# Fewer, larger pieces for the first and last loads of a decode attention kernel

## The chip, the cores and the metric

One core of a Trainium2 chip runs the kernel. The metric is device time in microseconds (us); less is better.

## The reference

One query for each of 16 heads attends to 8192 keys of width 256, all in bf16:

```
B, H, Sq, Sk, D = 1, 16, 1, 8192, 256
scores = einsum("bhqd,bhkd->bhqk", q, k) * D ** -0.5
p = softmax(scores, axis=-1)
out = einsum("bhqk,bhkd->bhqd", p, v)
```

K and V are 4 MB a head each, 134 MB together, and each byte is used once.

## The kernel before

A head's K and V lie in SBUF as 128 partitions of 64 rows: partition p holds rows 64p to 64p + 63, so that a "column" j (one of the 64) is one row of 256 numbers in each partition, 64 KB over all partitions. There are two buffers for K and two for V; even heads use the first, odd heads the second.

**Loads.** The list `stream` (lines 57 to 70) holds (K or V, head, first column, last column, semaphore) in the order of issue, and SP issues all of it on one queue (line 136). Before K of head h it waits until DVE has finished head h - 2 (line 133, semaphore `kd`), before V of head h until TensorE has finished the weighted sum of head h - 2 (line 135, `pv`). Heads 0 and 1 wait for nothing. A load in pieces has one semaphore for each piece. K0 comes as columns 0 to 15, 16 to 31 and 32 to 63. V0 and V1 come in halves, with K2 between the halves of V0 and K3 between the halves of V1. From head 2 on the list is K of head h + 2, then V of head h. V13 comes in halves, V14 in four pieces of 16 columns, V15 in nine pieces, the last two of 2 columns.

**Scores.** Of each head's 64 columns, DVE does the first 48 (`head`, lines 180 to 207): one multiply-and-sum a column (line 191), with a wait at the columns where a new piece of K0 begins (line 187). TensorE does the last 16 (`scores`): transposes (line 280), which ACT copies to SBUF (line 376), then matmuls with q (line 294). TensorE begins a head of even number only when all of K0 has come (lines 274 to 276). DVE then takes the maximum of each partition (line 207); TensorE transposes these (line 228), DVE takes the maximum of all (line 173), TensorE spreads it (line 234), and ACT takes the exponential (line 388). DVE's two small steps for other heads, `recips` and `xmax`, are put in between its columns (lines 217 and 218).

**Weighted sum.** `pv` (lines 252 to 269) is 64 matmuls, one a column of V, into one row of PSUM. It waits for the first piece of V, and at a column where a piece may begin it waits for that piece's semaphore. TensorE's code is a loop over pairs of heads with one body for all turns, so the waits for the pieces of V13, V14 and V15 stand in each turn. They compare with a register (`fin_turn`, `half_turn`, lines 348 and 349) that is 16 in all turns but the last, or last two, where it is 32; the semaphores start at 16, given by POOL (line 167). The order in a turn is scores of the even head, pv of the even head two before (with the small matmuls of the odd head in between at columns 32, 48 and 64), scores of the odd head, pv of the odd head two before (lines 351 to 366).

**Output.** ACT scales the row by the reciprocal of the sum (line 401) and issues its store (line 408).

Of the kernel before, what the change touches and what calls it, by code (L numbers as in the profile page):

```python
# [10 lines left out]

NPE = 16
GRP = 4
K_FIRST = (16, 32)
V_HALVED = 13
V_LATE = {14: (0, 16, 32, 48), 15: (0, 16, 28, 38, 46, 52, 57, 60, 62)}
AHEAD = {"kd": 1, "sc": 1, "sp": 2, "ex": 2, "m": 1, "g": 1, "mT": 1, "l": 2, "bc": 1, "nb": 1, "rc": 2, "pv": 2, "fin": 4}
V_SEMS = (("va0", "v0b", "v0c", "v0d"), ("va1", "v1b", "v1c", "v1d", "v1e", "v1f", "v1g", "v1i", "v1j"))


class _Step:
# [19 lines left out]
def bass_standalone__mha_softmax__decode_kernel(nc: bass.Bass, q: bass.AP, k: bass.AP, v: bass.AP, out: bass.AP):  # L41
    B, H, Sq, D = q.shape
    Sk = k.shape[2]
    P = 128
    J = Sk // P
# [3 lines left out]
    NG = NPE // GRP  # L49
    JD = J - NPE  # L50
    QW = D + NH
    HALF = J // 2
    dt = k.dtype

    stream = [("k", 0, 0, K_FIRST[0], "k0"), ("k", 0, K_FIRST[0], K_FIRST[1], "k0a")]
    stream += [("k", 0, K_FIRST[1], J, "k0b"), ("k", 1, 0, J, "k1")]
    stream += [("v", 0, 0, HALF, "va0"), ("k", 2, 0, J, "k0"), ("v", 0, HALF, J, "v0c")]
    stream += [("v", 1, 0, HALF, "va1"), ("k", 3, 0, J, "k1"), ("v", 1, HALF, J, "v1c")]  # L60
    for h in range(2, H):
        if h + 2 < H:
            stream.append(("k", h + 2, 0, J, f"k{h % 2}"))
        if h in V_LATE:
            for (a, b), name in zip(zip(V_LATE[h], V_LATE[h][1:] + (J,)), V_SEMS[h % 2]):
                stream.append(("v", h, a, b, name))
        elif h == V_HALVED:
            stream += [("v", h, 0, HALF, "va1"), ("v", h, HALF, J, "v1h")]
        else:
            stream.append(("v", h, 0, J, f"va{h % 2}"))  # L70

    with contextlib.ExitStack() as ctx:
# [39 lines left out]

        for name in ("qc", "pool", "cb", "cf", "qp", "qs", "qb", "kd", "tp", "kt", "sp", "sc", "m", "mT", "g", "bc", "nb", "ex"):
            sem(name)
        for name in ("l", "rc", "pv", "fin", "ldq", "k0", "k0a", "k0b", "k1", "va0", "va1", "v1h", "o0", "o1"):
            sem(name)
        late = [name for row in V_SEMS for name in row[1:] if name not in ("v0c", "v1c")] + ["v1h"]
        for row in V_SEMS:
            for name in row[1:]:
                sem(name)  # L120

        def src(t, h):
            return t[0, h].rearrange("(p j) d -> p (j d)", p=P)

        if True:
# [15 lines left out]
            @(lambda f: f(nc.gpsimd))  # L141
            def _(pool):
                def step(ins, n):
                    ins.then_inc(sem("pool"), 1)
                    pool.wait_ge(sem("pool"), n)

                def eye(t, n, done):
                    step(pool.memset(t[:, :], 0.0), n)
                    pool.affine_select(
                        out=t[:, :],  # L150
                        in_=t[:, :],
                        compare_op=ALU.not_equal,
                        fill=1.0,
                        base=0,
                        pattern=[[-1, P]],
                        channel_multiplier=1,
                    ).then_inc(sem(done), 1)

                eye(identb, 1, "cb")
                eye(ident, 2, "cf")  # L160
                pool.memset(ones_row[:, :], 1.0).then_inc(sem("cf"), 1)
                pool.memset(ones_col[:, :], 1.0).then_inc(sem("cf"), 1)
                pool.memset(q_all[:, H * QW : (H + 1) * QW], 0.0).then_inc(sem("cf"), 1)
                for name, n in AHEAD.items():
                    pool.nop().then_inc(sem(name), n)
                for name in late + ["o0", "o1", "va0", "va1"]:
                    pool.nop().then_inc(sem(name), 32 if name in ("o0", "o1") else 16)

            @(lambda f: f(nc.vector))
            def _(dve):  # L170
                def xmax(h):
                    dve.wait_ge(sem("mT"), h.of(1, 2))
                    dve.tensor_reduce(g[0:1, h.par : h.par + 1], mx[0:1, 0:P], AX.X, ALU.max).then_inc(sem("g"), 1)  # L173

                def recips(h):
                    dve.wait_ge(sem("l"), h.of(1, 3))
                    dve.wait_ge(sem("fin"), h.of(1, 3))
                    dve.reciprocal(recip[0:1, h.par : h.par + 1], qps[0:1, 0:1]).then_inc(sem("rc"), 1)  # L178

                def head(h, at):  # L180
                    dve.wait_ge(sem("qb"), h.of(1, 1))
                    dve.wait_ge(sem("ex"), h.of(1, 1))
                    dve.wait_ge(sem(f"k{h.par}"), h.of(8, 16 - 8 * h.par))  # L183
                    buf = kbuf[h.par]
                    for j in range(JD):
                        if j in K_FIRST and h.par == 0:
                            dve.wait_ge(sem("k0a" if j == K_FIRST[0] else "k0b"), 16)
                        if j == JD - 1:

                            dve.wait_ge(sem("sc"), h.of(1, 2))  # L190
                        ins = dve.tensor_tensor_reduce(  # L191
                            out=buf[:, j * D : (j + 1) * D],
                            in0=buf[:, j * D : (j + 1) * D],
                            in1=q_now[h.par][:, 0:D],
                            scale=SCALE,
                            scalar=0.0,
                            op0=ALU.mult,
                            op1=ALU.add,
                            accum_out=S[h.par][:, j : j + 1],
                        )  # L200
                        if j in at:
                            at[j]()
                    ins.then_inc(sem("kd"), 1)
                    if JD in at:
                        at[JD]()
                    dve.wait_ge(sem("kd"), h.of(1, 2))
                    dve.tensor_reduce(m[:, h.par : h.par + 1], S[h.par][:, :], AX.X, ALU.max).then_inc(sem("m"), 1)  # L207

                with dve.Fori(0, H // 2) as i:  # L209
                    ev, od = _Step(0, i), _Step(1, i)  # L210
                    prev = od.back(2)

                    def later(f, h):
                        with dve.If(i > 0):
                            f(h)

                    head(ev, {2: lambda: later(recips, ev.back(2)), 40: lambda: later(xmax, prev)})
                    head(od, {2: lambda: later(recips, prev), 3: lambda: xmax(ev)})
                last = _Step(H - 1)
                recips(last.back(1))  # L220
                xmax(last)
                recips(last)

            @(lambda f: f(nc.tensor))
            def _(pe):
# [23 lines left out]
                        stop=True,  # L249
                    ).then_inc(sem("l"), 1)  # L250

                def pv(h, waits, at):

                    pe.wait_ge(sem("fin"), h.of(1, 3))
                    pe.wait_ge(sem(f"va{h.par}"), h.of(8, 32 - 8 * h.par))
                    for j in range(J):
                        for name, value in waits.get(j, ()):
                            pe.wait_ge(sem(name), value)
                        ins = pe.matmul(  # L259
                            acc[h.par][0:1, 0:D],  # L260
                            lhsT=E[h.par][:, j : j + 1],
                            rhs=vbuf[h.par][:, j * D : (j + 1) * D],
                            start=(j == 0),
                            stop=(j == J - 1),
                        )
                        if j == J - 1:
                            ins.then_inc(sem("pv"), 1)
                        if j + 1 in at:
                            at[j + 1]()
# [75 lines left out]
                pe.wait_ge(sem("cf"), 4)  # L345
                with pe.Fori(0, H // 2 + 1) as i:
                    ev, od = _Step(0, i), _Step(1, i)
                    fin_turn = pe.snap((i // 8) * 16 + 16)
                    half_turn = pe.snap(((i + 1) // 8) * 16 + 16)
                    old = od.back(2)  # L350
                    with pe.If(i < H // 2):
                        scores(ev)
                    with pe.If(i > 0):
                        pv(
                            ev.back(2),
                            {V_LATE[14][n]: [(V_SEMS[0][n], fin_turn)] for n in range(1, len(V_SEMS[0]))},
                            {32: lambda: transpose_m(old), 48: lambda: bcast(old), 64: lambda: total(old)},
                        )
                    with pe.If(i < H // 2):
                        scores(od, before=ev)  # L360
                    with pe.If(i > 0):
                        waits = {V_LATE[15][n]: [(V_SEMS[1][n], fin_turn)] for n in range(1, len(V_SEMS[1]))}
                        waits[HALF] = [("v1h", half_turn)]
                        pv(old, waits, {})
                    with pe.If(i < H // 2):
                        total(ev)

# [121 lines left out]
```

## Time and profile before

| | us |
|---|---|
| median of 3 runs | 320.18 (320.08 to 320.52) |
| the profiled execution | 320.12 |
| its span, first to last instruction | 318.6 |
| busy, DVE | 275.2 |
| busy, TensorE matmuls | 219.2 |
| busy, ACT | 92.5 |
| mean DMA rate over the span | 421 GB/s read |

The span is told from the profile of one execution, whose own time stands beside it. Busy times overlap. In the timeline a row has the start in us, how long it took, the engine, the line, what it writes and reads, how many instructions are taken together, and in brackets how long the engine had been idle and what ended that. "PEld" is TensorE's weight loads, "SPq" and "ACTq" are the issues of DMAs on those engines' queues. In the DMA view a queue's row has packets, MB, and the time of the packets as a share of 16 engines' time; an issue's row has KB and us from the issue to the landing.

### The profile page before, as it was taken

Reading aid. Unit: us, or ns where it says so; the run is one execution under the profiler, and the core shown is the slowest. Engines: PE = TensorE matmul, PEld = TensorE weight load, DVE = VectorE, ACT = ScalarE, POOL = GpSimd, SP = SyncE. Lnnn points to the kernel's source line nnn. Section 1 sums busy time; section 2 is a strip of 40 time slices with the busy share of each in tenths; the row PEclk is TensorE's granted clock in tenths of the full one; section 3 lists DMA queues with packets and bytes.
Section 4 is the critical chain, followed back from the end, with each engine's and each line's share of the span. In section 5 each row is a group of like instructions: output and inputs, shape, how many; then the busy total and the mean of one; then the engine's idle time right before and its main releaser. Section 6 shows DMA issues by size and latency. Waiting matters only on the chain.

```text
span 318.6 us, 6833 instructions
## 1 busy us (share of the span) xinstructions
PE 219.2 (69%) x2163; PEld 156.0 (49%) x2163; DVE 275.2 (86%) x1584; ACT 92.5 (29%) x172; POOL 1.6 (0%) x11
## 2 busy tenths in 40 slices
PE   4446185988775947949387482975739668497987
PEld 1335163656553634727256262663626446266664
DVE  3989999999999898897988979799798897979920
ACT  5436050333215050330505114051330603306010
POOL 1000000000000000000000000000000000000000
PEclk9999999659797875957879597695977859699999
DMA  7999999999999999999999999999999999999995
GB/s 303 447 418 465 393 455 407 448 416 448 412 448 428 428 444 411 453 412 453 420 436 440 416 448 407 453 416 449 424 432 444 411 449 416 444 405 428 419 416 201
DMA packets 6981, 134.29 MB, mean 422 GB/s; under 512 B 800, under 2 KB 1216, under 8 KB 1856
## 3 DMA queue, kind: packets, MB, share of 16 engines
q1 hardware_dynamic: 6912, 134.22, 98.6%
q8 instruction: 2, 0.03, 0.0%
q10 hardware_dynamic: 64, 0.02, 0.0%
q14 instruction: 3, 0.02, 0.0%
HBM read 134.23 MB, written 0.01 MB: 421 GB/s over the span
## 4 chain that ended last, share of the span: by engine, by line
DMA 64%; PE 19%; DVE 15%; SPq 1%; issue 1%; ACT 0%; DVEq 0%; ACTq 0%
DMA vbuf<-in_v_dram 58%; PE acc L259 18%; DVE kbuf L191 14%; DMA kbuf<-in_k_dram 7%; SPq L136 1%; DVE S L191 0%; DVE g L173 0%; PE sm L234 0%; ACT o_sb L401 0%; DVE recip L178 0%; DVEq L209 0%; DVEq L183 0%; PE qps L244 0%; DVE m L207 0%; ACTq L400 0%
## 5 line engine op out<-in xcount | busy, mean ns | idle before, releaser
L191 DVE CUSTOM_DVE_ANT_0 kbuf<-kbuf,q_now 128x256 bf16<-128x256 bf16 x768 | 268.4, 409 | 21.3 <-DMA kbuf<-in_k_dram 20.4
L259 PE MATMUL acc<-vbuf,E 128*1 128x256 bf16 x1024 | 147.1, 313 | 41.6 <-DMA vbuf<-in_v_dram 41.4
L259 PEld LDWEIGHTS acc<-vbuf,E 128*1 128x1 bf16 x1024 | 95.5, 95 | 86.2 <-DMA vbuf<-in_v_dram 44.4
L376 ACT ACTIVATE KT<-tp 128x1024 bf16<-128x1024 bf16 x64 | 62.3, 1021 | 46.4 <-PE tp L280 45.9
L191 DVE DVE_READ_ACCUMULATOR2_ANT S<- 128x1 f32 x768 | 55.2, 72 | 0.0
L280 PE MATMUL tp<-identb,kbuf 128*128 128x128 bf16 x512 | 42.2, 239 | 14.7 <-DMA kbuf<-in_k_dram 14.5
L280 PEld LDWEIGHTS tp<-identb,kbuf 128*128 128x128 bf16 x512 | 33.6, 107 | 18.1 <-DMA kbuf<-in_k_dram 12.1
L294 PE MATMUL spe<-q_now,KT 128*128 128x1 bf16 x512 | 22.9, 166 | 27.3 <-ACT KT L376 27.0
L294 PEld LDWEIGHTS spe<-q_now,KT 128*128 128x128 bf16 x512 | 18.1, 99 | 35.7 <-ACT KT L376 26.1
L401 ACT ACTIVATE o_sb<-acc,recip 1x256 bf16<-1x256 f32 x16 | 7.3, 458 | 87.0 <-PE acc L259 85.7
L384 ACT ACTIVATE negb<-sm 128x1 f32<-128x1 f32 x16 | 2.8, 174 | 83.8 <-PE sm L234 83.8
L173 DVE TENSOR_REDUCE g<-mx 1x1 f32<-1x128 f32 x16 | 4.4, 276 | 7.5 <-PE mx L228 7.5
L234 PE MATMUL sm<-g,ones_row 1*128 1x1 f32 x32 | 6.5, 268 | 5.0 <-DVE g L173 5.0
L228 PE MATMUL mx<-ident,m 128*1 128x128 f32 x32 | 6.5, 287 | 4.3 <-DVE m L207 4.3
L234 PEld LDWEIGHTS sm<-g,ones_row 1*128 1x128 f32 x32 | 5.1, 198 | 7.1 <-DVE g L173 5.6
L371 ACT ACTIVATE q_now<-q_all 128x258 bf16 x16 | 6.7, 418 | 0.1
L178 DVE RECIPROCAL recip<-qps 1x1 f32<-1x1 f32 x16 | 2.4, 152 | 3.9 <-PE qps L244 3.9
L388 ACT ACTIVATE E<-S,negb 128x64 bf16<-128x64 f32 x16 | 5.6, 348 | 0.5
L336 PE MATMUL acc<-q_sb,identb 16*128 16x256 bf16 x16 | 4.3, 404 | 0.8 <-ACT q_all L426 0.8
L228 PEld LDWEIGHTS mx<-ident,m 128*1 128x1 f32 x32 | 2.1, 82 | 5.1 <-DVE m L207 4.8
L426 ACT ACTIVATE q_all<-acc 128x512 bf16<-128x512 f32 x8 | 4.3, 592 | 0.6 <-PE acc L336 0.6
L380 ACT ACTIVATE S<-spe 128x16 f32<-128x16 f32 x16 | 2.9, 184 | 3.6 <-PE spe L294 3.6
(24 smaller groups left out, 18.5 us busy)
## 6 DMA issues: line engine op xcount, KB each, us to landing
kbuf<-in_k_dram SPq DMA_DIRECT2D x15, 4096.0 KB, 20.3
vbuf<-in_v_dram SPq DMA_DIRECT2D x11, 4096.0 KB, 28.7
vbuf<-in_v_dram SPq DMA_DIRECT2D x6, 2048.0 KB, 24.4
vbuf<-in_v_dram SPq DMA_DIRECT2D x5, 1024.0 KB, 14.8
kbuf<-in_k_dram SPq DMA_DIRECT2D x2, 1024.0 KB, 5.8
kbuf<-in_k_dram SPq DMA_DIRECT2D x1, 2048.0 KB, 11.3
vbuf<-in_v_dram SPq DMA_DIRECT2D x1, 768.0 KB, 10.2
vbuf<-in_v_dram SPq DMA_DIRECT2D x1, 640.0 KB, 11.3
```

The lines of the kernel that those rows point to most:

```text
L173: dve.tensor_reduce(g[0:1, h.par : h.par + 1], mx[0:1, 0:P], AX.X, ALU.max).then_inc(sem("g"), 1)
L191: ins = dve.tensor_tensor_reduce(out=buf[:, j * D : (j + 1) * D], in0=buf[:, j * D : (j + 1) * D], in1=q_now[h.par][:, 0:D], scale=SCALE, ...
L228: pe.matmul(mx[0:1, 0:P], lhsT=m[:, h.par : h.par + 1], rhs=ident[:, :], start=True, stop=True).then_inc(sem("mT"), 1)
L234: pe.matmul(sm[:, 0:1], lhsT=ones_row[0:1, 0:P], rhs=g[0:1, h.par : h.par + 1], start=True, stop=True,).then_inc(sem("bc"), 1)
L259: ins = pe.matmul(acc[h.par][0:1, 0:D], lhsT=E[h.par][:, j : j + 1], rhs=vbuf[h.par][:, j * D : (j + 1) * D], start=(j == 0), stop=(j == J ...
L280: ins = pe.transpose(tp[gi % 2][:, b * D + hf * P : b * D + (hf + 1) * P], buf[:, j * D + hf * P : j * D + (hf + 1) * P], identb[:, :],)
L294: ins = pe.matmul(spe[:, c : c + 1], lhsT=KT[gi % 2][:, b * D + hf * P : b * D + (hf + 1) * P], rhs=q_now[h.par][:, D + hf : D + hf + 1], ...
L336: ins = pe.matmul(acc[pair % 2][:, (h % 2) * D : (h % 2 + 1) * D], lhsT=identb[0:H, h : h + 1].to_broadcast([H, P]), rhs=q_sb[:, :], start ...
L371: act.activation(out=q_now[h.par][:, :], in_=src_q, func=ACT.Copy).then_inc(sem("qb"), 1)
L376: act.activation(out=KT[gi % 2][:, :], in_=tp[gi % 2][:, :], func=ACT.Copy).then_inc(sem("kt"), 1)
L388: act.activation(out=E[h.par][:, :], in_=S[h.par][:, :], func=ACT.Exp, bias=negb[:, h.par : h.par + 1], scale=1.0, accum_out=lsum[:, h.par ...
L401: act.activation(out=o_sb[h.par][0:1, :], in_=acc[h.par][0:1, 0:D], func=ACT.Copy, scale=recip[0:1, h.par : h.par + 1],).then_inc(sem("fin ...
```

## The change

The first and last loads are cut differently. K0 comes as columns 0 to 15 and 16 to 63. V0 and V1 come whole, so that the list begins K0 (two pieces), K1, V0, K2, V1, K3, K4, V2, K5, V3. V13 comes in 34 and 30 columns, V14 in 24, 20 and 20, V15 in 20, 14, 10, 8, 6, 4 and 2. The waits for pieces compare with the constant 16 in all turns: POOL gives each of their semaphores 16 for each turn but those in which a load gives it, and the first matmul of each piece takes 16 back. The registers `fin_turn` and `half_turn` go.

```
-K_FIRST = (16, 32)
-V_HALVED = 13
-V_LATE = {14: (0, 16, 32, 48), 15: (0, 16, 28, 38, 46, 52, 57, 60, 62)}
+K_FIRST = 16
+V_LATE = {13: (0, 34), 14: (0, 24, 44), 15: (0, 20, 34, 44, 52, 58, 62)}
+V_SEMS = {13: ("va1", "v1c"), 14: ("va0", "v0b", "v0c"), 15: ("va1", "v1b", "v1c", "v1d", "v1e", "v1f", "v1g")}
...
-    stream = [("k", 0, 0, K_FIRST[0], "k0"), ("k", 0, K_FIRST[0], K_FIRST[1], "k0a")]
-    stream += [("k", 0, K_FIRST[1], J, "k0b"), ("k", 1, 0, J, "k1")]
-    stream += [("v", 0, 0, HALF, "va0"), ("k", 2, 0, J, "k0"), ("v", 0, HALF, J, "v0c")]
-    stream += [("v", 1, 0, HALF, "va1"), ("k", 3, 0, J, "k1"), ("v", 1, HALF, J, "v1c")]
+    stream = [("k", 0, 0, K_FIRST, "k0"), ("k", 0, K_FIRST, J, "k0b"), ("k", 1, 0, J, "k1")]
+    stream += [("v", 0, 0, J, "va0"), ("k", 2, 0, J, "k0"), ("v", 1, 0, J, "va1"), ("k", 3, 0, J, "k1")]
...
+        late = {}
+        for h, names in V_SEMS.items():
+            for name in names[1:]:
                 sem(name)
+                late[name] = late.get(name, 16 * H // 2) - 16
...
-                        if j in K_FIRST and h.par == 0:
-                            dve.wait_ge(sem("k0a" if j == K_FIRST[0] else "k0b"), 16)
+                        if j == K_FIRST and h.par == 0:
+                            dve.wait_ge(sem("k0b"), 16)
...
+                    parts = dict(zip(V_LATE[H - 2 + h.par][1:], V_SEMS[H - 2 + h.par][1:]))
...
                     for j in range(J):
-                        for name, value in waits.get(j, ()):
-                            pe.wait_ge(sem(name), value)
+                        if j in parts:
+                            pe.wait_ge(sem(parts[j]), 16)
                         ins = pe.matmul(
...
                         )
+                        if j in parts:
+                            ins.then_inc(sem(parts[j]), -16)
```

More of the change, by code (lines that the diff above doesn't have):

```diff
@@ L13 @@
 GRP = 4
-K_FIRST = (16, 32)
-V_HALVED = 13
-V_LATE = {14: (0, 16, 32, 48), 15: (0, 16, 28, 38, 46, 52, 57, 60, 62)}
+K_FIRST = 16
+V_LATE = {13: (0, 34), 14: (0, 24, 44), 15: (0, 20, 34, 44, 52, 58, 62)}
+V_SEMS = {13: ("va1", "v1c"), 14: ("va0", "v0b", "v0c"), 15: ("va1", "v1b", "v1c", "v1d", "v1e", "v1f", "v1g")}
 AHEAD = {"kd": 1, "sc": 1, "sp": 2, "ex": 2, "m": 1, "g": 1, "mT": 1, "l": 2, "bc": 1, "nb": 1, "rc": 2, "pv": 2, "fin": 4}
-V_SEMS = (("va0", "v0b", "v0c", "v0d"), ("va1", "v1b", "v1c", "v1d", "v1e", "v1f", "v1g", "v1i", "v1j"))
 class _Step:
@@ L51, in bass_standalone__mha_softmax__decode_kernel @@
     QW = D + NH
-    HALF = J // 2
     dt = k.dtype
-    stream = [("k", 0, 0, K_FIRST[0], "k0"), ("k", 0, K_FIRST[0], K_FIRST[1], "k0a")]
-    stream += [("k", 0, K_FIRST[1], J, "k0b"), ("k", 1, 0, J, "k1")]
-    stream += [("v", 0, 0, HALF, "va0"), ("k", 2, 0, J, "k0"), ("v", 0, HALF, J, "v0c")]
-    stream += [("v", 1, 0, HALF, "va1"), ("k", 3, 0, J, "k1"), ("v", 1, HALF, J, "v1c")]
+    stream = [("k", 0, 0, K_FIRST, "k0"), ("k", 0, K_FIRST, J, "k0b"), ("k", 1, 0, J, "k1")]
+    stream += [("v", 0, 0, J, "va0"), ("k", 2, 0, J, "k0"), ("v", 1, 0, J, "va1"), ("k", 3, 0, J, "k1")]
     for h in range(2, H):
@@ L64, in bass_standalone__mha_softmax__decode_kernel @@
         if h in V_LATE:
-            for (a, b), name in zip(zip(V_LATE[h], V_LATE[h][1:] + (J,)), V_SEMS[h % 2]):
+            for (a, b), name in zip(zip(V_LATE[h], V_LATE[h][1:] + (J,)), V_SEMS[h]):
                 stream.append(("v", h, a, b, name))
-        elif h == V_HALVED:
-            stream += [("v", h, 0, HALF, "va1"), ("v", h, HALF, J, "v1h")]
         else:
@@ L114, in bass_standalone__mha_softmax__decode_kernel @@
             sem(name)
-        for name in ("l", "rc", "pv", "fin", "ldq", "k0", "k0a", "k0b", "k1", "va0", "va1", "v1h", "o0", "o1"):
+        for name in ("l", "rc", "pv", "fin", "ldq", "k0", "k0b", "k1", "va0", "va1", "o0", "o1"):
             sem(name)
-        late = [name for row in V_SEMS for name in row[1:] if name not in ("v0c", "v1c")] + ["v1h"]
-        for row in V_SEMS:
-            for name in row[1:]:
+        late = {}
+        for h, names in V_SEMS.items():
+            for name in names[1:]:
                 sem(name)
+                late[name] = late.get(name, 16 * H // 2) - 16
         def src(t, h):
@@ L165, in _ @@
                     pool.nop().then_inc(sem(name), n)
-                for name in late + ["o0", "o1", "va0", "va1"]:
-                    pool.nop().then_inc(sem(name), 32 if name in ("o0", "o1") else 16)
+                for name, n in list(late.items()) + [("o0", 32), ("o1", 32), ("va0", 16), ("va1", 16)]:
+                    pool.nop().then_inc(sem(name), n)
             @(lambda f: f(nc.vector))
@@ L250, in total, with pv @@
                     ).then_inc(sem("l"), 1)
-                def pv(h, waits, at):
+                def pv(h, at):
+                    parts = dict(zip(V_LATE[H - 2 + h.par][1:], V_SEMS[H - 2 + h.par][1:]))
                     pe.wait_ge(sem("fin"), h.of(1, 3))
@@ L347, in _ @@
                     ev, od = _Step(0, i), _Step(1, i)
-                    fin_turn = pe.snap((i // 8) * 16 + 16)
-                    half_turn = pe.snap(((i + 1) // 8) * 16 + 16)
                     old = od.back(2)
@@ L355, in _ @@
                             ev.back(2),
-                            {V_LATE[14][n]: [(V_SEMS[0][n], fin_turn)] for n in range(1, len(V_SEMS[0]))},
                             {32: lambda: transpose_m(old), 48: lambda: bcast(old), 64: lambda: total(old)},
@@ L361, in _ @@
                     with pe.If(i > 0):
-                        waits = {V_LATE[15][n]: [(V_SEMS[1][n], fin_turn)] for n in range(1, len(V_SEMS[1]))}
-                        waits[HALF] = [("v1h", half_turn)]
-                        pv(old, waits, {})
+                        pv(old, {})
                     with pe.If(i < H // 2):
```

## The prediction

> **What bounds the kernel now.** I read the head of the page and its list of queues first, then the issues of the SP queue in the timeline, then the landing of single transfers (the DMA view cut to one issue each), and last the waits of DVE and TensorE beside them.
>
> ```profile
> span 318.6 us, 6833 instructions
> q1 hardware_dynamic: 6912, 134.22, 98.6%
> ```
>
> All K and V, 134.22 MB, go through one queue whose packets fill 98.6% of the 16 DMA engines' time. The reader is to see that no compute engine can be the bound while that holds: what counts is how many bytes, what each transfer costs beside its bytes, whether the queue ever runs empty, and what is left to do after the last byte. The profiled execution took 320.12 us, its span 318.6, so 1.5 us lie around the span; the median of the three runs is 320.18, 0.06 above it. I add my sum to the median.
>
> The pace of the stream, from TensorE's waits:
>
> ```profile
> 82.60 5.02 PE L259 MATMUL acc<-vbuf,E 128*1 128x256 bf16 x32 [0.97 <-DMA vbuf<-in_v_dram]
> ...
> 102.04 9.03 PE L259 MATMUL acc<-vbuf,E 128*1 128x256 bf16 x64 [2.75 <-DMA vbuf<-in_v_dram]
> ...
> 111.76 1.07 PE L280 MATMUL tp<-identb,kbuf 128*128 128x128 bf16 x16 [0.66 <-DMA kbuf<-in_k_dram]
> ```
>
> V2 has landed at 82.60, V3 at 102.04, K6 at 111.76: 19.44 us for two heads' worth of 4 MB, 9.72 for one, so 0.152 us for a column of 64 KB.
>
> And the issues, with the landings behind them:
>
> ```profile
> 0.74 2.03 SPq L136 DMA_DIRECT2D kbuf<-in_k_dram  x4
> ...
> 22.26 0.33 SPq L136 DMA_DIRECT2D kbuf<-in_k_dram  x1
> 22.63 1.79 SPq L136 DMA_DIRECT2D vbuf<-in_v_dram  x2
> 40.27 0.33 SPq L136 DMA_DIRECT2D kbuf<-in_k_dram  x1
> 40.64 0.43 SPq L136 DMA_DIRECT2D vbuf<-in_v_dram  x1
> 57.96 0.33 SPq L136 DMA_DIRECT2D kbuf<-in_k_dram  x1
> 59.69 0.33 SPq L136 DMA_DIRECT2D vbuf<-in_v_dram  x1
> 75.69 0.33 SPq L136 DMA_DIRECT2D kbuf<-in_k_dram  x1
> ...
> 93.36 0.33 SPq L136 DMA_DIRECT2D kbuf<-in_k_dram  x1
> ```
>
> The K rows are K2, K3, K4, K5 and K6, each issued when DVE has done the head two before. The answers for V0's second half (issued 22.63), V1's second half (40.64) and V2 (59.69), in this order, count us from issue to landing:
>
> ```profile
> vbuf<-in_v_dram SPq DMA_DIRECT2D x1, 2048.0 KB, 21.0
> ...
> vbuf<-in_v_dram SPq DMA_DIRECT2D x1, 2048.0 KB, 22.5
> ...
> vbuf<-in_v_dram SPq DMA_DIRECT2D x1, 4096.0 KB, 22.9
> ```
>
> They land at 43.6, 63.1 and 82.6. I call **cover** the time from an issue to the landing of what is queued ahead of it. K4 has 63.1 - 58.0 = 5.2 us of it, K5 82.6 - 75.7 = 6.9: the queue never empties.
>
> **Part 1: fewer transfers.** Before there are 48 loads of K and V: 18 of K, 30 of V. After, K0 comes in two instead of three, V0 and V1 in one instead of two, V14 in three instead of four, V15 in seven instead of nine, V13 still in two: 42. What one costs beside its bytes is read from the last V, whose pieces TensorE waits for:
>
> ```profile
> 308.84 1.61 PEld L259 LDWEIGHTS acc<-vbuf,E 128*1 128x1 bf16 x16 [0.65 <-DMA vbuf<-in_v_dram]
> 310.74 1.18 PEld L259 LDWEIGHTS acc<-vbuf,E 128*1 128x1 bf16 x12 [0.28 <-DMA vbuf<-in_v_dram]
> 312.32 0.96 PEld L259 LDWEIGHTS acc<-vbuf,E 128*1 128x1 bf16 x10 [0.41 <-DMA vbuf<-in_v_dram]
> 313.62 0.74 PEld L259 LDWEIGHTS acc<-vbuf,E 128*1 128x1 bf16 x8 [0.34 <-DMA vbuf<-in_v_dram]
> 314.63 0.52 PEld L259 LDWEIGHTS acc<-vbuf,E 128*1 128x1 bf16 x6 [0.27 <-DMA vbuf<-in_v_dram]
> 315.41 1.18 PEld L259 LDWEIGHTS acc<-vbuf,E 128*1 128x1 bf16 x12 [0.26 <-DMA vbuf<-in_v_dram]
> 316.97 0.47 ACT L401 ACTIVATE o_sb<-acc,recip 1x256 bf16<-1x256 f32 x1 [8.15 <-PE acc L259]
> 317.47 0.24 ACTq L408 DMA_DIRECT2D out_dram<-o_sb  x1
> ```
>
> Twelve columns take 310.74 - 308.84 = 1.90 us, ten 1.58, eight 1.30, six 1.01. At 0.152 a column that leaves 0.08, 0.06, 0.08 and 0.10 for the transfer itself. Six fewer save 0.4 to 0.6; at the low end, 0.07, since three of the six are large and these rows are of small ones: **-0.4 us**, all of it on the path, since the stream is the path.
>
> **Part 2: the tail.** TensorE takes about 0.1 us a column (12 in 1.18, 10 in 0.96), less than the stream's 0.152, so each piece is worked off while the next lands, if the next isn't much smaller. New order 20, 14, 10, 8, 6, 4, 2: 20 columns take 2.0 while 14 land in 2.2; 14 take 1.4 against 1.6; 10, 1.0 against 1.3; 8, 0.8 against 1.0; 6, 0.6 against 0.7; 4, 0.4 against 0.37. Only there TensorE is 0.03 behind, and 2 columns follow as before. Nothing else stands in the tail: the copy of 0.47 and the output are the same. I put **+0.1 us**, with 0 and +0.3 as ends (the higher if the larger steps cost a wait each, 0.05 for six).
>
> The amount taken back from a semaphore rides on one matmul a piece; the register waits that it replaces go. No row shows such a matmul. It is bounded by nothing from below and by a weight load's 0.1 us from above, and only the last two lie in the tail: in the 0.3 above. The Trainium skill speaks against it: "TensorE: Matmul & The Clock Gate", section "The cost: per-tile semaphore tail", has updates of a semaphore by matmuls serialize at 26.3 ns each; by that the six of the last V would cost an estimated 0.16 us, the two in the tail 0.05. No run here shows it.
>
> **Part 3: the order at the start.** Here covers shrink.
>
> ```profile
> 5.54 0.42 DVE L191 CUSTOM_DVE_ANT_0 kbuf<-kbuf,q_now 128x256 bf16<-128x256 bf16 x1 [5.54 <-DMA kbuf<-in_k_dram]
> ...
> 40.99 0.43 DVE L191 CUSTOM_DVE_ANT_0 kbuf<-kbuf,q_now 128x256 bf16<-128x256 bf16 x1 [0.49 <-issue]
> ...
> 58.41 0.43 DVE L191 CUSTOM_DVE_ANT_0 kbuf<-kbuf,q_now 128x256 bf16<-128x256 bf16 x1 [0.23 <-DMA kbuf<-in_k_dram]
> ...
> 59.74 0.16 DVE L178 RECIPROCAL recip<-qps 1x1 f32<-1x1 f32 x1 [0.20 <-PE qps L244]
> ```
>
> TensorE's first transposes, which wait for all of K0, and the issue of K3 (40.27) with its us to landing:
>
> ```profile
> 13.03 1.86 PE L280 MATMUL tp<-identb,kbuf 128*128 128x128 bf16 x16 [3.96 <-DMA kbuf<-in_k_dram]
> ...
> kbuf<-in_k_dram SPq DMA_DIRECT2D x1, 4096.0 KB, 18.0
> ```
>
> Head 0: DVE starts at 5.54 and a head takes some 17.0 us for 48 columns (40.99 to the issue of K4 at 57.96), 0.35 each. It has done 16 by 11.1 and now waits for all of K0, 13.0: +1.9. K2 goes out at 24.1 instead of 22.26, but V0 whole lies ahead of it: plenty. Head 1 ends 1 to 2 us later, at 41 to 42, and K3 goes out then, behind all of V1.
>
> Head 2: K2 now lands behind K0, K1 and all of V0, the bytes that ended at 43.6 before, less two transfers: 43.5. DVE begins 0.15 later (it began K3, landed at 58.27, at 58.41) and ends 16.97 on: K4 is issued at **60.6**, not 57.96. Ahead of it lies K3 alone, at the byte count that ended at 63.1, less three transfers: 62.9. Cover **2.3 us**.
>
> Head 3: DVE starts at 62.9 + 0.15; 58.41 to 75.69 less the wait of 0.20 is 17.1; K5 goes out at **80.15**. V2 lands at 82.6 - 0.2 = 82.4. Cover **2.2 us**. Afterwards V3 lies between again: K6 goes out near 97.8 against V3's landing at 101.8, 4 us, and later heads gain. V2 itself, which waits for TensorE's first pv, moves with head 2, 59.69 to 62.4, ten us ahead of need; V3 stays right behind K5.
>
> Is 2.2 enough? What counts is the time from an issue to packets. The DMA view of short stretches shows it:
>
> ```profile
> DMA packets 0, 0.00 MB, mean 0 GB/s; under 512 B 0, under 2 KB 0, under 8 KB 0
> ...
> q1 hardware_dynamic: 12, 0.10, 224.6%
> ...
> q1 hardware_dynamic: 8, 0.07, 40.8%
> ```
>
> No packet from 0 to 1.7 us, 12 from 1.7 to 2.0, 8 more to 2.7: on a quiet chip 1.0 us after the issue at 0.74 for the first of the 16 DMA engines, some 1.9 for the last.
>
> ```profile
> 100.37 0.23 ACTq L408 DMA_DIRECT2D out_dram<-o_sb  x1
> ```
> ```profile
> q1 hardware_dynamic: 50, 1.51, 100.0%
> ...
> q10 hardware_dynamic: 1, 0.00, 0.8%
> ```
>
> In the middle of the stream an output issued at 100.37 has no packet up to 103.8 but for one just there (the first row is 100.3 to 103.8, q10 absent; the second 103.8 to 104): 3.4 us. And a landing is told some 0.4 us after its packet: the last output's packets start after 318.1 and the span ends at 318.6. So the packets of K3 and V2 end 0.4 before the landings, and a cover of 2.2 bears 1.8 us. The stream loses (latency - 1.8), once, since a loss at K4 delays V2 as much and lengthens K5's cover: **0 at 1.0, 1.6 at 3.4**. It can't gain. I take the middle, 2.4: at both places the queue is full when the issue goes out and empties while it is under way. **+0.6 us**.
>
> **Sum**: -0.4 + 0.1 + 0.6 = +0.3: 320.5 us. The cut of V13 is free:
>
> ```profile
> 300.10 4.12 SPq L136 DMA_DIRECT2D vbuf<-in_v_dram  x9
> ```
>
> V15 goes out when pv of head 13 is done, which now has 30 columns left after its last piece, not 32: 0.2 earlier, with the rest of V14 (landed near 308.84 less 16 columns, 306.3) 6 us ahead of it.
>
> **Rivals.**
> 1. The quiet latency holds (1.0 to 1.9): no loss, -0.3, 319.9. For it: most DMA engines are idle by then. Against: the 3.4. The Trainium skill stands here: "DMA: Bandwidth & Descriptors", section "Specifications", gives about 0.6 us to the first byte for these queues; by that 319.9 too. This case's trace has 1.0 at the least.
> 2. **Slower**: at K4 and K5 the stream stands for the whole loaded latency, 2.9 to 3.5, a loss of 1.1 to 1.7: 321.0 to 321.6. It decides from a latency of 2.7 on. For it: the 3.4 of the output; against: that is another queue, sharing with full ones.
> 3. A transfer costs its bytes alone and the tail's 0.3 comes due: +0.3 + 0.6, 321.1.
> 4. Faster: instruction fetches fall on a DMA engine in the stream, as here from 22.2 to 22.6:
>
> ```profile
> q8 instruction: 1, 0.02, 15.9%
> ```
>
> 15.9% of 16 engines' 0.4 us is 1.0 us of one engine; the program is shorter, and if the latest engine loses one fetch, and nothing is lost at K4 and K5, 318.9, or 319.4 if half of it counts.
>
> **Chances.** Forecast (320.2 to 320.9) 0.34, rival 1 0.26, rival 2 0.30, rival 3 0.05, rival 4 0.05. The range leaves out rival 4 and the top of rival 2: 319.6 to 321.5. A measurement tells 0.2%, 0.64 us, from no change. Slower: rivals 2 and 3 and 0.03 of the forecast, 0.38. Faster: rival 4 and 0.01 of rival 1, 0.06. Same: 0.56.
>
> **What would show it.** 42 loads; K4 issued near 60.6 and K5 near 80.15, K3 and V2 landed near 62.9 and 82.4; K5's landing 9.7 us after V2's if nothing is lost, up to 11.3 if rival 2 holds; the output's copy 0.5 to 0.6 us after the last landing. I am wrong if DVE's heads 2 and 3 don't start with their K, or if a landing in the steady part stretches.

## The result and the profile after

The changed kernel takes **320.47 us** in the median of 14 runs (320.19 to 322.11); the kernel before, run beside it 14 times, 320.12 (320.05 to 320.52). The medians differ by 0.35 us, the means (320.87 and 320.15) by 0.7; the ratio over the runs is **1.0023**, 95% interval 1.0014 to 1.0032. Mean and ratio lie above the medians because the runs of the changed kernel fall into two groups: nine between 320.19 and 320.77, five between 321.49 and 322.11, none between. No run of the kernel before is over 320.52. I call a run **late** if it takes over 321.0.

The profiled execution took 320.42, one of the nine. The head of its page and its queue of loads:

```profile
span 318.9 us, 6865 instructions
q1 hardware_dynamic: 6048, 134.22, 98.4%
```

The same 134.22 MB went in 6048 packets instead of 6912. Both are 144 a load, so 42 loads instead of 48. The stream of loads is the bound as before.

SP's issues in the timeline:

```profile
24.18 0.33 SPq L131 DMA_DIRECT2D kbuf<-in_k_dram  x1
...
41.24 19.71 SPq L131 DMA_DIRECT2D kbuf<-in_k_dram  x2
60.99 0.43 SPq L131 DMA_DIRECT2D vbuf<-in_v_dram  x1
80.18 0.33 SPq L131 DMA_DIRECT2D kbuf<-in_k_dram  x1
...
97.85 0.33 SPq L131 DMA_DIRECT2D kbuf<-in_k_dram  x1
```

K2, K3 with K4, V2, K5 and K6. The row with x2 joins two issues: it ends at 41.24 + 19.71 = 60.95, and an issue takes 0.33, so K4 went out at **60.62**. K5 went out at **80.18**. DVE's rows say why:

```profile
43.65 0.42 DVE L185 CUSTOM_DVE_ANT_0 kbuf<-kbuf,q_now 128x256 bf16<-128x256 bf16 x1 [2.19 <-DMA kbuf<-in_k_dram]
...
63.21 0.43 DVE L185 CUSTOM_DVE_ANT_0 kbuf<-kbuf,q_now 128x256 bf16<-128x256 bf16 x1 [2.36 <-DMA kbuf<-in_k_dram]
```

Heads 2 and 3 begin with the landing of their K, after idle times of 2.19 and 2.36 us that the kernel before did not have there. The us from issue to landing of K4, V2 and K5, from the DMA view cut to each issue:

```profile
kbuf<-in_k_dram SPq DMA_DIRECT2D x1, 4096.0 KB, 12.2
...
vbuf<-in_v_dram SPq DMA_DIRECT2D x1, 4096.0 KB, 21.5
...
kbuf<-in_k_dram SPq DMA_DIRECT2D x1, 4096.0 KB, 12.2
```

K4 landed 60.62 + 12.2 = 72.8, V2 at 82.5, K5 at 92.4. A landing is the last of 16 semaphore updates, one from each DMA engine. Read to 0.01 us from the trace, against the kernel before at the same count of bytes (at K2 and K3 its row has the landings of the second halves of V0 and V1, which end there):

```
            K0     K1     K2     K3     K4     V2     K5     K6     V13    last
before    12.89  23.21  43.64  63.14  72.84  82.56  92.28 111.71 296.37  316.45
after     12.97  23.24  43.63  63.05  72.79  82.50  92.38 111.88 296.54  316.54
after-bef +0.08  +0.03  -0.01  -0.09  -0.05  -0.06  +0.10  +0.17  +0.17   +0.09
```

In this run the stream is 0.09 early at K3, loses 0.04 at K4, 0.16 at K5 and 0.07 by K6, and wins 0.08 in the last two V. The covers, the time from an issue to the landing of what is queued ahead, were 63.05 - 60.62 = 2.4 at K4 and 82.50 - 80.18 = 2.3 at K5.

At K4 the stream did run partly dry, as the DMA view of 61 to 64 us shows for the kernel before and for the changed one:

```profile
DMA packets 54, 1.36 MB, mean 453 GB/s; under 512 B 9, under 2 KB 9, under 8 KB 9
```
```profile
DMA packets 39, 1.11 MB, mean 371 GB/s; under 512 B 5, under 2 KB 5, under 8 KB 5
```

A quarter of a MB is missing, 0.25 MB / 0.43 MB per us = 0.6 us of the stream, and yet K4 landed 0.04 late. The 16 parts of each landing (its semaphore updates, one from each DMA engine) show where it went. Us behind the first part, sorted, with the second half of V1 for K3 of the kernel before:

```
before  V1b 0 .05 .15 .16 .17 .23 .29 .30 .31 .32 .36 .37 1.12 1.70 1.76 1.93
before  K4  0 .04 .15 .17 .23 .29 .31 .32 .33 .36 .37 .55 1.12 1.69 1.75 1.91
after   K3  0 .15 .16 .22 .28 .30 .31 .36 .37 .38 .43 .63 1.12 1.66 1.81 2.17
after   K4  0 .02 .12 .13 .14 .15 .16 .17 .18 .22 .24 .25  .41  .44  .47  .48
after   K5  0 .23 .25 .26 .29 .37 .38 .39 .40 .40 .41 .42  .44  .45  .49  .62
```

At K3 the first twelve engines end 1.5 to 2.2 us ahead of the last; that spread builds up over the first 44 us, in which five instruction fetches of 0.3 to 1.1 us fall on single engines. At K4 the median part goes from 61.25 to 72.49, 11.24 us instead of 9.7: the twelve lose about 1.5 us. Their last packets of K3 end at 60.4 to 61.1 and their first ones of K4 start at 61.6 to 61.9, so a little more than half of it is idle; the rest is that these first packets take 1.7 to 2.1 us instead of 1.21. But the landing goes by the last engine, which still had packets. In this run the lead of the others is spent there: V2's parts are within 0.5 us. At K5 hardly an engine stands idle, but thirteen of the 16 first packets take 1.28 to 1.57 us, and that is the 0.16.

The tail, TensorE's weight loads and ACT:

```profile
313.41 0.99 PEld L254 LDWEIGHTS acc<-vbuf,E 128*1 128x1 bf16 x10 [0.16 <-issue]
314.70 0.77 PEld L254 LDWEIGHTS acc<-vbuf,E 128*1 128x1 bf16 x8 [0.31 <-issue]
315.68 0.55 PEld L254 LDWEIGHTS acc<-vbuf,E 128*1 128x1 bf16 x6 [0.20 <-issue]
316.38 0.55 PEld L254 LDWEIGHTS acc<-vbuf,E 128*1 128x1 bf16 x6 [0.15 <-issue]
```
```profile
317.31 0.47 ACT L393 ACTIVATE o_sb<-acc,recip 1x256 bf16<-1x256 f32 x1 [7.00 <-PE acc L254]
317.81 0.24 ACTq L400 DMA_DIRECT2D out_dram<-o_sb  x1
```

The last piece landed at 316.54 and the copy starts at 317.31, 0.77 later; before it was 316.97 - 316.45 = 0.52. The idle time before a piece is now put down to "issue", not to the DMA: the wait is an instruction of its own (EVENT_SEMAPHORE in the trace) ahead of the weight load.

### The profile page after: what moved, and what is told of

The parts are those of the page before. It is cut to its first block, busy times and chain, and to the rows that moved or that the text cites. A ratio compares the mean times of both kernels' runs of the same rounds, so it can differ in the third digit from the quotient of the medians.

```text
span 318.9 us, 6865 instructions
## 1 busy us (share of the span) xinstructions
PE 220.6 (69%) x2163; PEld 157.2 (49%) x2163; DVE 275.1 (86%) x1584; ACT 92.6 (29%) x172; POOL 1.6 (0%) x11
## 3 DMA queue, kind: packets, MB, share of 16 engines
q1 hardware_dynamic: 6048, 134.22, 98.4%
## 4 chain that ended last, share of the span: by engine, by line
DMA 46%; DVE 28%; PE 22%; issue 2%; ACT 1%; SPq 0%; DVEq 0%; ACTq 0%
DMA vbuf<-in_v_dram 36%; DVE kbuf L185 27%; PE acc L254 20%; DMA kbuf<-in_k_dram 11%; DVE S L185 1%; PE sm L228 1%; ACT KT L368 1%; PE mx L222 0%; PE tp L277 0%; DVE g L168 0%; PE spe L291 0%; SPq L131 0%; ACT o_sb L393 0%; DVE recip L173 0%; DVEq L203 0%
## 5 line engine op out<-in xcount | busy, mean ns | idle before, releaser
L254 PEld LDWEIGHTS acc<-vbuf,E 128*1 128x1 bf16 x1024 | 96.5, 96 | 78.6 <-DMA vbuf<-in_v_dram 34.3
L393 ACT ACTIVATE o_sb<-acc,recip 1x256 bf16<-1x256 f32 x16 | 7.3, 458 | 81.4 <-PE acc L254 80.2
```

What stands on the lines that cost most here:

```text
L254: ins = pe.matmul(acc[h.par][0:1, 0:D], lhsT=E[h.par][:, j : j + 1], rhs=vbuf[h.par][:, j * D : (j + 1) * D], start=(j == 0), stop=(j == J ...
L393: act.activation(out=o_sb[h.par][0:1, :], in_=acc[h.par][0:1, 0:D], func=ACT.Copy, scale=recip[0:1, h.par : h.par + 1],).then_inc(sem("fin ...
```

## Experiments

Covers are read from one profiled execution of each kernel. All but e4 start from the changed kernel. The kernel before had medians of 320.18, 320.17 and 320.14 beside the three groups (76 runs, 319.95 to 320.47).

### e1, V0 and V1 in halves again, all else as changed

```
-    stream += [("v", 0, 0, J, "va0"), ("k", 2, 0, J, "k0"), ("v", 1, 0, J, "va1"), ("k", 3, 0, J, "k1")]
+    cut = {0: "h0b", 1: "h1b"}
+    stream += [("v", 0, 0, 32, "va0"), ("k", 2, 0, J, "k0"), ("v", 0, 32, J, "h0b")]
+    stream += [("v", 1, 0, 32, "va1"), ("k", 3, 0, J, "k1"), ("v", 1, 32, J, "h1b")]
...
+                        if j == 32 and h.par in cut:
+                            pe.wait_ge(sem(cut[h.par]), 16)
```

> The changed kernel with V0 and V1 in halves again, K2 and K3 between the halves; the rest, the new last pieces and their waits too, stays. Theory (short covers at K4 and K5): K4 goes out near 59 with some 4 us or more queued ahead, K5 likewise; no packet gap there, all runs within 0.3 us of each other and within 0.3 us of the kernel before (-0.3 for four loads fewer, +0.25 for the longer tail). Rival 'tail and waits': as the changed kernel, +0.3 and single runs up to +1.9. Rival 'instruction fetches' (two fetches on one DMA engine in some runs): late runs stay, about one in three by 1.2 or more.

Measured: 320.07 (319.96 to 320.42, 11 runs), ratio 0.9999, 0.9991 to 1.0008; none late. SP's issues of K4 and K5, and their us to landing:

```profile
58.77 0.33 SPq L135 DMA_DIRECT2D kbuf<-in_k_dram  x1
...
76.50 0.33 SPq L135 DMA_DIRECT2D kbuf<-in_k_dram  x1
```
```profile
kbuf<-in_k_dram SPq DMA_DIRECT2D x1, 4096.0 KB, 14.0
...
kbuf<-in_k_dram SPq DMA_DIRECT2D x1, 4096.0 KB, 15.7
```

Covers are 4.3 and 6.0 us, K4 lands at 72.8 and K5 at 92.2. The runs lie within 0.46 us, not 0.3, but none is over what the kernel before reached (320.52). The late runs go with the whole V0 and V1, not with the tail, the first K or the take-back.

### e2 and e3, one of the two in halves

Each has one half of e1's edit: e2 cuts V0 and leaves V1 whole, e3 the reverse.

```
e2: cut = {0: "h0b"}
e3: cut = {1: "h1b"}
```

> The changed kernel with V0 in halves and V1 whole: K2 lands early, so K4 is issued near 59 with 4 us queued ahead, while K5 keeps its 2.2 us. Theory: the gap at K4 goes, the one at K5 stays; between 0 and +1.3 us over the kernel before, run to run. If K4 alone made the loss: within 0.3 us of the kernel before in all runs.

> The changed kernel with V0 whole and V1 in halves: K4 keeps its 2.3 us of cover (issued near 60.6), K3 lands five us earlier, so K5 goes out near 78.4 with 4 us ahead. Theory: a gap at K4 alone; between 0 and +1.3 us over the kernel before, run to run. If K5 alone made the loss: within 0.3 us of the kernel before in all runs.

e2: 321.32 (320.42 to 321.55, 6 runs), ratio 1.0028, 1.0016 to 1.0040; four of six late. e3: 320.31 (320.16 to 321.83, 11 runs), ratio 1.0011, 1.0002 to 1.0020; one of eleven late. e2's K5 in SP's issues and in the DMA view:

```profile
80.11 0.33 SPq L135 DMA_DIRECT2D kbuf<-in_k_dram  x1
```
```profile
kbuf<-in_k_dram SPq DMA_DIRECT2D x1, 4096.0 KB, 13.3
```

K5 lands at 93.45, 10.8 us after V2 (82.64), where the stream's step is 9.7: 1.1 us lost at one place. e2 has a cover of 4.2 at K4 and 2.5 at K5, e3 2.5 at K4 and 4.8 at K5. So the short cover at K5 costs, and that at K4 hardly does: in e3 two of eleven runs lie over 320.6, at 320.79 and 321.83.

### e4, the kernel before with whole V0 and V1 alone

```
-    stream += [("v", 0, 0, HALF, "va0"), ("k", 2, 0, J, "k0"), ("v", 0, HALF, J, "v0c")]
-    stream += [("v", 1, 0, HALF, "va1"), ("k", 3, 0, J, "k1"), ("v", 1, HALF, J, "v1c")]
+    stream += [("v", 0, 0, J, "va0"), ("k", 2, 0, J, "k0"), ("v", 1, 0, J, "va1"), ("k", 3, 0, J, "k1")]
```

> The kernel before with V0 and V1 whole as the only change: its last pieces, register waits and K0 in three stay. Theory: the late runs stay (some of the runs +1.0 or more over the kernel before), the early ones come to -0.1 to +0.1, as the longer tail is gone. Rival 'tail and waits': all runs within 0.2 us of the kernel before.

Measured: 321.25 (320.32 to 321.93, 11 runs), ratio 1.0029, 1.0018 to 1.0041; seven of eleven late, with the old tail, the old waits and K0 in three pieces. The four others lie 0.1 to 0.3 over the kernel before, not within 0.1 as expected. With e1 this ends the rival that the tail and its waits make the late runs. The profiled run, 321.08, loses its time at another place than e2's, though. K4 and K5 in the DMA view:

```profile
kbuf<-in_k_dram SPq DMA_DIRECT2D x1, 4096.0 KB, 12.3
...
kbuf<-in_k_dram SPq DMA_DIRECT2D x1, 4096.0 KB, 12.4
```

Both land 9.9 us after what is ahead of them and lose 0.2 each. K2 was 0.73 late already (44.37 against 43.64), its parts 2.79 us apart instead of 2.17: one part of K0's first piece came 0.84 us behind the first (0.38 in the kernel before), and the last part fell back by 1 us more at K1 and again at K2, about what an instruction fetch of 16 KB takes. That the same engine had two fetches is read out of these steps; the trace does not name the engines.

### e5, e6 and e7, K3 or K2 in halves, V0 and V1 whole

DVE can begin head 3 with the first half of K3 and so issue K5 earlier (e5), head 2 with the first half of K2 and so issue K4 earlier (e6); e7 does both. Each second half has its own semaphore, which DVE waits for in mid-head and TensorE before its transposes.

```
e5: ("k", 3, 0, J, "k1")  ->  ("k", 3, 0, 32, "k1"), ("k", 3, 32, J, "k3b")
e6: ("k", 2, 0, J, "k0")  ->  ("k", 2, 0, 32, "k0"), ("k", 2, 32, J, "k2b")
e7: both
```

> The changed kernel, V0 and V1 whole, with K3 in two halves, so that DVE begins head 3 when head 2 is done (61.3) and K5 goes out near 78.4 instead of 80.2: some 4 us queued ahead of it; K4 keeps 2.3. All up to 60 us stays as in the changed kernel. Theory (the loss is at K5): within 0.3 us of the kernel before and at most one late run in ten. Rival 'instruction fetches', which fall around 35 us in the changed kernel: late runs by over 1 us stay, about one in three.

> The changed kernel with K2 in two halves: K4 goes out near 59 with 4 us ahead, K5 near 80.2 with 2.2. Theory: late runs by about 1 us stay and are the majority, as with V0 in halves, since the DMA engines are then not brought into step at K4 before K5 comes late. Rival 'K4 is the place': within 0.3 us of the kernel before, no late run.

> K2 and K3 both in halves, V0 and V1 whole: both covers near 4 us. Theory: no late run, within 0.2 us of the kernel before. Rival 'instruction fetches' or 'whole V0 and V1 as such': late runs stay, one in three or more.

| | cover at K4 | cover at K5 | median (lowest to highest, runs) | ratio, 95% | late |
|---|---|---|---|---|---|
| e5 | 2.5 | 5.4 | 320.17 (319.96 to 320.78, 11) | 1.0002, 0.9993 to 1.0011 | 0 |
| e6 | 4.4 | 2.3 | 320.82 (320.21 to 322.57, 10) | 1.0027, 1.0013 to 1.0041 | 4 |
| e7 | 3.7 | 6.0 | 320.36 (320.03 to 321.24, 11) | 1.0005, 0.9996 to 1.0014 | 1 |

Three expectations were missed: e7 was to have no late run and has one, e6 was to have a majority and has four of ten, and e5's slowest run is 0.6 above the kernel before, not within 0.3.

The issues of K3 (in two) with K4, of V2 and of K5 in e5, then K5's in e6:

```profile
41.22 19.61 SPq L134 DMA_DIRECT2D kbuf<-in_k_dram  x3
60.87 0.43 SPq L134 DMA_DIRECT2D vbuf<-in_v_dram  x1
77.62 0.33 SPq L134 DMA_DIRECT2D kbuf<-in_k_dram  x1
```
```profile
80.18 0.33 SPq L134 DMA_DIRECT2D kbuf<-in_k_dram  x1
```

e5 leaves K4 at 41.22 + 19.61 - 0.33 = 60.50 and moves K5 alone by 2.6 us; no run is late. e6 moves K4 alone; four of ten are. This repeats e2 and e3 by another means, and with a load more instead of fewer: how often runs are late goes with the issue of K5 against V2's landing, not with the number or shape of the loads. K4's short cover can still cost a little: in e5's profile K4 lands 10.34 us after K3, 0.6 late. Why K5 is the worse place is not shown. The lead of the twelve engines is not the reason: in e6, where K4 has cover, V2's first twelve parts still end 1.6 to 2.0 us ahead of the last, much as those ahead of K4 do in e3 and e5 (1.4 to 2.2), at about the same cover, and yet four of ten runs are late against one of 22. The one profile of e6 is of an early run; it loses 0.62 at K5 (its step is 10.33).

### e8 and e9, attempts at a better kernel

e8 is e1 with the small pieces of before at the end of V15, and the amount taken back by a piece's second matmul. e9 is e7 with K0 in three pieces again.

```
e8: 15: (0, 20, 34, 44, 52, 57, 60, 62)
e8: done = j if j == J - 2 else j - 1
    if done in parts and j < J - 1:
        ins.then_inc(sem(parts[done]), -16)
e9: ("k", 0, 0, 16, "k0"), ("k", 0, 16, 32, "k0a"), ("k", 0, 32, J, "k0b")
```

> V0 and V1 in halves as in the first experiment, and a finer tail: V15 in 20, 14, 10, 8, 5, 3, 2 and 2 columns, and the amount taken back by the second matmul of a piece, so that the wait may ride on the first one's weight load. Theory: the tail is 0.2 us shorter than in the first experiment: 0.1 to 0.4 us faster than the kernel before. Rival (more pieces eat it): as the first experiment, within 0.1 of the kernel before.

> As K2 and K3 in halves with V0 and V1 whole, but K0 in three pieces as in the kernel before, so that DVE doesn't wait 1.9 us in head 0: K4 and K5 go out a us earlier, with 5 us queued ahead of each instead of 4. Theory (a load that goes out with 5 us of cover loses nothing, one with 4 sometimes 0.6): all runs within 0.4 us of the kernel before, none later. Rival (whole V0 and V1 as such, or the taking back): spread as with the K halves alone, single runs 0.8 or more late.

e8: 320.15 (319.96 to 320.82, 11 runs), ratio 1.0002, 0.9993 to 1.0011, none late. It was to win 0.1 to 0.4 us and won nothing that can be told. Its profiled run, 320.56, lost 0.6 at K4 with a cover of 4.0. The tail is shorter than the changed kernel's: the last piece lands at 316.91 and ACT's copy follows 0.60 later. Where the second matmul takes the amount back, the wait rides on the weight load again (the idle time before it is put down to the DMA), and ten weight loads take 0.96 us as in the kernel before:

```profile
313.72 0.96 PEld L260 LDWEIGHTS acc<-vbuf,E 128*1 128x1 bf16 x10 [0.18 <-DMA vbuf<-in_v_dram]
...
317.51 0.47 ACT L400 ACTIVATE o_sb<-acc,recip 1x256 bf16<-1x256 f32 x1 [7.34 <-PE acc L260]
```

e9: 320.25 (320.02 to 320.70, 11 runs), ratio 1.0003, 0.9994 to 1.0012, none late. Its cover at K4 was to be 5 us and was 4.0 (issue 59.13, K3 landed 63.17), since head 2 took a us longer (DVE stands 1.07 us in it for TensorE's transposed maxima of head 1); so it does not tell whether 5 us would do. Its slowest run is 0.56 above the kernel before, not within 0.4. No version beats the kernel before.

### e10, e11 and e12, the changed kernel again

Nothing is edited: three more profiled executions, to catch late ones and see where they lose.

> The changed kernel again, for a second profile. Theory: if this run is late (over 321.2), K5 lands 10.5 us or more after V2 instead of 9.7, and nothing else is longer by over 0.4; if it is early (320.2 to 320.8), K5 lands within 10.1 us of V2. Rival 'instruction fetches': a late run has the last of K3's 16 parts over 2.5 us behind the first, and K5 on time.

> The changed kernel again, for a third profile; expected as for the second.

> The changed kernel again, for a fourth profile; expected as for the second.

All three were late: 321.62, 322.11 and 321.33. The DMA view for K4, V2 and K5 of e11, then for K4 and K5 of e12:

```profile
kbuf<-in_k_dram SPq DMA_DIRECT2D x1, 4096.0 KB, 13.9
...
vbuf<-in_v_dram SPq DMA_DIRECT2D x1, 4096.0 KB, 23.4
...
kbuf<-in_k_dram SPq DMA_DIRECT2D x1, 4096.0 KB, 14.1
```
```profile
kbuf<-in_k_dram SPq DMA_DIRECT2D x1, 4096.0 KB, 12.2
...
kbuf<-in_k_dram SPq DMA_DIRECT2D x1, 4096.0 KB, 13.4
```

In e11 and e12 the issues of K4 and K5 stand within 0.06 us of those in the first profile. In e12 K4 takes the same 12.2 us and K5 1.2 more: its step from V2 is 11.03 us, a loss of 1.3. In e11 it is K4 that loses: 13.9, a step of 11.45, so 1.74 lost. V2 then lands at 84.4, K5's cover becomes 84.4 - 80.2 = 4.2, and K5's step is 9.90. e10 loses 0.75 by K2, as e4 did (44.38, parts 2.88 apart), and 0.68 at K5. The expectation that the loss sits at K5 alone is therefore wrong: it is K5 in e12 and e2, K4 in e11, and half of e10's falls before either, as most of e4's does.

What differs inside is one DMA engine. The steady 32 KB packet takes 1.21 us. In the first profile the first packets of K4 start 0.96 to 1.84 us after the issue and take 1.5 to 2.1 us on all engines but the last, which had packets of K3 until then; in e11 15 engines do much the same, and one starts 2.6 us after the issue with a packet of 2.5 us. That engine ends 1.7 to 2.0 us behind the next one, and 2.3 to 2.5 behind the first, from K4 to V4. In e12 the last engine starts on K5 at 83.0, 2.9 after the issue, and in e2 2.6 after it.

All runs together, by cover (short is 2.5 us or less):

| short cover | kernels | late runs |
|---|---|---|
| at neither | before, e1, e7, e8, e9 | 1 of 134 |
| at K4 alone | e3, e5 | 1 of 22 |
| at K5 alone | e2, e6 | 8 of 16 |
| at both | changed, its three repeats, e4 | 15 of 28 |

The line at 321.0 suits the changed kernel, whose runs leave a gap there; e6's spread from 320.21 to 322.57, with a gap of only 0.43 there. With a line at 320.7 the rows would read 2, 3, 11 and 16, so the order does not hang on it. The rows count lateness of any cause: what e4 and e10 lost by K2 is no matter of the covers at K4 and K5.

The rival that instruction fetches, moved by the new program, fall on a bad place holds for neither e11 nor e12: the five fetches run at 18.2, 23, 35.1, 35 to 36 and 37.3 us in the early profile as in these. It may hold for the lateness by K2 in e4 and e10.

## Why the prediction was right, and where its steps were not

The forecast of +0.3 came out (+0.35 in the medians, +0.30 in the profiled executions), but in good part by luck: its three terms, -0.4, +0.1 and +0.6, measured -0.17, +0.25 and +0.27 in the first profile, and the errors cancel.

**The places** were right: K2 24.1 (24.18), K4 60.6 (60.62), K5 80.15 (80.18), K6 97.8 (97.85); K3 and V2 landed at 63.05 and 82.50 against 62.9 and 82.4, and the covers were 2.4 and 2.3 against 2.3 and 2.2. This chain (whole V0 delays K2, K2 delays DVE, DVE delays K4 and K5) is what e1, e2, e3, e5 and e6 take apart, and each moves the issue as it says. V2 went out at 60.99, not 62.4: it was held only by K4 ahead of it on SP. Nothing followed.

**Fewer transfers, -0.4**, were -0.17 in the first profile: 0.09 by K3 and 0.08 in the last two V. The price of 0.07 was read from pieces of 6 to 12 columns; V14 in three instead of four wins 0.07. But whole V0 and V1 win little: e1, with both in halves again, reaches the count of bytes of K3 at 63.06, the first profile, e11 and e12, with both whole, at 63.00 to 63.05. And the two pieces that went from V15 were of the smallest. Its landings, as us from the one before, with the columns:

```
before  16: 2.48  12: 1.89  10: 1.59  8: 1.30  6: 1.01  5: .78  3: .46  2: .30  2: .32   sum 10.13
after   20: 3.12  14: 2.19  10: 1.59  8: 1.29  6:  .97  4: .70  2: .27                   sum 10.13
```

At 0.152 a column the last three pieces before cost 0.00 to 0.02 beside their bytes. In this pair of profiles two loads fewer there save nothing; in e10, e11 and e12 the seven pieces take 10.04 to 10.08, so 0.05 to 0.09 less, and the last two V together win 0.14 to 0.17. K0 in two instead of three can't be told: it landed at 12.97 against 12.89, but over all profiles with two pieces at 12.64 to 13.30.

**The tail, +0.1**, was +0.25. The first part is as worked out, only larger: the last 2 columns land 0.27 after the 4, which TensorE works off in some 0.43, so it is 0.16 behind, not 0.03. The rest, about 0.1, is the step that the prediction bounded by a weight load's 0.1 and left inside its 0.3: the wait stands in the trace as an instruction of its own, and the weight load begins 0.08 after it, where before it rode on the weight load. The rows of pieces are 0.03 longer too (ten weight loads take 0.99 against 0.96, eight 0.77 against 0.74, six 0.55 against 0.52), but that goes with the separate wait as well: the first weight load of a piece then stands 0.03 ahead of its matmul, and in e8, where the second matmul takes the amount back without such a wait, ten take 0.96 again. The Trainium skill, "TensorE: Matmul & The Clock Gate", section "The cost: per-tile semaphore tail", gives 26.3 ns for each increment by a matmul; no row here shows such a cost of the update itself.

**The restart, +0.6**, is where the number came out right for a reason that was only half right. That the covers at K4 and K5 get too short and that this is the main risk of the change, the experiments show. But the loss was taken as one latency, 2.4 us between 1.0 and 3.4, less a cover of 1.8. (Two of its figures are off: the middle of 1.0 and 3.4 is 2.2, which gives +0.4; and in the trace the last of the 16 first packets starts at 2.24, 1.5 us after the issue at 0.74, not 1.9, since four of the eight packets up to 2.7 are second ones.) The runs show no one value: with a short cover 0.04 and 0.16 us were lost at K4 and K5 in the first profile, 0.6 to 0.7 at K4 in e5 and at K5 in e6 and e10, 1.1 to 1.7 at one of them in e2, e11 and e12. The small loss of rival 1 and the large one of rival 2 both happen, in different runs (rival 1's time of 319.9 does not: the fastest run took 320.19). The median, in the upper part of the first group, is near the forecast by luck, without its mechanism. Two things were missing. A landing waits for the slowest of 16 engines, and before K4 the first twelve have 1.5 to 2.2 us of lead to lose; in the first profile that hid 1.5 us. And most engines start 1.0 to 1.8 us after the issue, with a slow first packet, but now and then one starts at 2.6 to 2.9. The Trainium skill's 0.6 us to the first byte ("DMA: Bandwidth & Descriptors", section "Specifications") is under all of them; the earliest packet of K4 in the first profile came 0.96 us after its issue.

**Only once**: right. In e11 the loss at K4 gives K5 a cover of 4.2, and K5 loses 0.2.

Summed for the first profile: -0.17 from the loads, +0.04, +0.16 and +0.07 at K4, K5 and K6, +0.25 in the tail is +0.35, against 318.92 - 318.57 = +0.35 of the spans and 320.42 - 320.12 = +0.30 of the executions. Rivals 3 (a transfer costs its bytes alone) and 4 (one instruction fetch fewer) fall: the loads did save a little, and the fetches stayed at five.

What stays open is why one DMA engine at times gets its first packet 2.6 to 2.9 us after the issue (seen in e2, e11 and e12), why a short cover at K5 makes so many more runs late than one at K4, and how many of the late runs that were not profiled lost their time by K2, as e4 and e10 did. In those two one engine is 0.8 to 0.9 us behind at K0 already; so it is in e7 and e8, where only 0.35 us and nothing was lost by K2, and e8 has V0 and V1 in halves.

## What to carry to other kernels

Where one queue of loads is the bound, work out for each load that waits for a buffer how long before the landing of the load ahead it is issued; here 2.3 to 2.5 us at K5 went with 23 late runs of 44 (mostly 1 to 2 us), the same at K4 alone with one of 22, 3.7 us and more at both with one of 44, and 5.2 and 6.9 us with none of 90. A merge of loads that looks like less work can shorten that margin several heads later, through the engine that frees the buffer. And when a cost depends on the last of 16 engines, look at the spread over single runs and at two or three profiles, since a median can lie between two outcomes.

## What the runs showed of the hardware

- After a nearly dry queue the first 32 KB packet of all DMA engines but one takes 1.5 to 2.1 us instead of 1.21 (first profile, K4); at K5 thirteen of 16 take 1.3 to 1.6, and up to 2.7 was seen even with a cover of 4.3 us (e1, K4); with 5.2 us (before) none there took over 1.38.
- The 16 engines of one queue drift apart and stay apart: from 44 us on the last is 1.9 us behind the first in the kernel before, after 0.4 at K0, and in between five instruction fetches of 8 KB (0.31 to 0.43 us) and 16 KB (1.0 to 1.1 us) fall on single engines. The gap at K4 brought the spread from 2.17 to 0.48 us for a loss of 0.04 (first profile), but cost 1.7 in e11.
- In the changed kernel the wait before a matmul that also lowers the semaphore is an instruction of its own, and the weight load begins 0.08 us after it; with the lowering put on the next matmul (e8) the wait rides on the weight load as in the kernel before.
